# Loading q and k in longer runs, two batches per transfer, with both heads' scores over 128 rows of contraction

## Chip, core and metric

The kernel runs on one core of one Trainium2 chip. The metric is the time of one execution on the device, in microseconds (us); lower is better. TensorE multiplies matrices into PSUM; VectorE and ScalarE move results from PSUM to SBUF and compute on them; GpSimd issues nearly all loads from HBM, and SyncE the rest.

## What is computed

Selective attention over 8 batches of 8 heads, 576 tokens, 64 channels a head, and on its result a spectral mixing layer. All inputs are float32. Cut to what matters:

```python
# attention, per batch and head: q, k, v are [576, 64], s is [576]
scores = q @ k.T / 8
cum = np.cumsum(np.maximum(s, 0.0))
scores = np.where(causal, -1e9, scores + np.minimum(-(cum[:, None] - cum[None, :]), 0.0))
attn = softmax(scores)
x[b, :, 64 * head : 64 * head + 64] = attn @ v

# mixing, per batch: x is [576, 512], 64 modes, each with two 512x512 weights
X = rfft(x, axis=tokens)[:64]
Y = X @ (w_r + 1j * w_i)              # a matrix for each mode
u = x + irfft(Y)
out = u + np.maximum(u @ w_ch, 0.0)
```

The weights are the bulk of what is read: 2 x 64 matrices of 512x512. The type is converted from float32 to bfloat16 or float16 by the load itself, so that a load writes half of the bytes that it reads.

## The kernel before

**Steps.** Attention runs in 32 steps n. A step is one batch b and one pair of heads g (n = 8 g + b). What a step needs is loaded ahead: q and k of both heads, and v. The lists of loads are written in program order, one list per step: list n holds q, k and v of step n + 3 (`LA = 3`) and about five tiles of mixing weights. `load` merges the two kinds evenly into one order, and GpSimd issues them one after another. A weight tile is two transfers of 256 KB (bytes written), one for each half of the 128 partitions (L214). The first eight weight tiles lie in buffers that are needed for something else only later; the others go round two rings of 11 and 6 buffers (`WA`, `WB`; from tile 76 on the ring of 11 alone). A weight tile may be loaded when the matmuls that read the tile before it in its buffer are over.

**q and k.** `loads_qkv(n)` loads q in one transfer into `q2`, [128 partitions, 9 tokens, 64 channels]: each head takes 64 partitions, and a partition holds a run of 9 tokens, 1152 bytes as bfloat16. k goes to `k2` in the same way. The pool holds four such pairs.

**Transposes.** The scores need q and k with the channels on the partitions. `transposes(n, 0)` does q of both heads, `transposes(n, 1)` k: 9 x 2 TensorE transposes of 64x64 into one PSUM tile (there is one, so that the second call waits for the copies of the first), then two copies of 64x576 into SBUF. Head A's channels land in rows 0 to 63 of `qtA`, `ktA`, head B's in rows 64 to 127 of `qtB`, `ktB`. Three of the four copies are on VectorE, the last (`ktB`) on ScalarE (L335). There are two buffers of each, used in turn.

**Scores.** The bias enters as one more row of contraction: row 64 of `qtA` and row 0 of `qtB` hold minus 8 times the running sum (`cum_rows`, two small loads on SyncE's queue per step), and the same row of `ktA`, `ktB` holds ones. Head A contracts over 65 rows, head B over 128, of which 63 are zeros. `scores(n, h)` first adds the causal mask by a matmul (L368), then the products (L374), and ScalarE takes the exponential (L382). `scores4` does the last 64 tokens of both heads.

**The rest of a step.** `av` multiplies with v and divides by the row sums (x_all), `fft` transforms along the tokens, and `modes` multiplies with the weights (L452), one group of four weight tiles at a time, in steps 8 and later. The order of work on TensorE in step n is

```python
cum_rows(n + 1)
scores(n, 0); av(n - 1, 1); transposes(n + 1, 0)
scores(n, 1); transposes(n + 1, 1); fft(n - 1); av(n, 0)
for c in mode_steps.get(n, []): modes(...)
```

with products with `w_ch` among it in the last six steps. After attention come the remaining weights of the last channel group, with `modes` as they land, and then the inverse transform, the product with `w_ch`, relu and the stores.

Of the kernel before, what the change touches and what calls it, by code (L numbers as in the profile page):

```python
# [11 lines left out]
BF16 = mybir.dt.bfloat16  # L12
# [6 lines left out]
def kernel(  # L19
# [11 lines left out]
    nc = tc.nc  # L31
# [3 lines left out]
    P = 128  # L35
# [15 lines left out]
    NF = NT - 1  # L51
    R = S // (P // 2)
    RP = P // 2
    W = 2 * P
# [58 lines left out]
    ap_ = at.enter_context(tc.tile_pool(name="attn", bufs=1))  # L113
    qkpool = at.enter_context(tc.tile_pool(name="qk_sb", bufs=LA + 1))
    cumt_sb = ap_.tile([P, NK + 1, NPAIR], FP32, name="cumt_sb")
    cumt4 = ap_.tile([P, NPAIR // 2], FP32, name="cumt4")
    ncum_sb = ap_.tile([NPAIR, S], BF16, name="ncum_sb")
    NQ = 2
    qtA = [ap_.tile([NCH, S], BF16, name=f"qtA{i}") for i in range(NQ)]
    qtB = [ap_.tile([P, S], BF16, name=f"qtB{i}") for i in range(NQ)]  # L120
    ktA = [ap_.tile([NCH, S], BF16, name=f"ktA{i}") for i in range(NQ)]
    ktB = [ap_.tile([P, S], BF16, name=f"ktB{i}") for i in range(NQ)]
    NV = LA + 2
# [22 lines left out]

    def loads_qkv(n):

        if n >= N:
            return []  # L150
        g, b = divmod(n, B)
        hs = slice(2 * g, 2 * g + 2)
        q2 = qkpool.tile([P, R + 1, D], BF16, name="q2", tag="q2")[:, :R, :]
        k2 = qkpool.tile([P, R + 1, D], BF16, name="k2", tag="k2")[:, :R, :]
        loaded[n] = (q2, k2)
        todo = [
            (dst, src[b, hs].rearrange("h (p r) d -> (h p) r d", r=R))
            for src, dst in ((q, q2), (k, k2))
        ]
        todo += [  # L160
            (
                v2[n % NV][:, : 2 * NWN * W].rearrange("p (w h c) -> p w h c", w=NWN, h=2)[:, :, h, P:],
                v[b, 2 * g + h, : NF * P, :].rearrange("(w p r) d -> p w (r d)", p=P, r=2),
            )
            for h in range(2)
        ]
        return todo

# [85 lines left out]
    nc.sync.dma_start(out=negm32, in_=d_negm)  # L254
    first, second, tails0 = loads_qkv(0), loads_qkv(1), loads_tails(0)
    load(first[:2])
    load(loads_w(W0), first[2:] + tails0 + second)
    nc.sync.dma_start(out=Ff_sb, in_=d_Ff.rearrange("(T p) c -> p T c", p=P))
# [6 lines left out]
    for i in range(NQ):  # L265
        nc.vector.memset(qtB[i][0:64, :], 0.0)
        nc.vector.memset(ktB[i][0:64, :], 0.0)
        nc.vector.memset(ktB[i][0:1, :], 1.0)
        nc.vector.memset(ktA[i][D : D + 1, :], 1.0)
    for i in range(NV):  # L270
# [44 lines left out]
    def cum_rows(n):  # L315
        if n >= N:
            return
        g, b = divmod(n, B)
        p0 = b * H + 2 * g
        nc.sync.dma_start(out=qtA[n % NQ][D : D + 1, :], in_=ncum_sb[p0 : p0 + 1, :])  # L320
        nc.sync.dma_start(out=qtB[n % NQ][0:1, :], in_=ncum_sb[p0 + 1 : p0 + 2, :])

    def transposes(n, which):
        if n >= N:
            return
        src = loaded[n][which]
        dA, dB = ((qtA, qtB), (ktA, ktB))[which]
        g, b = divmod(n, B)
        ps = trpool.tile([P, R, RP], BF16, name="tr_ps", tag="tr")
        for r in range(R):  # L330
            for h in range(2):
                rows = slice(D * h, D * h + D)
                nc.tensor.transpose(ps[rows, r, :], src[rows, r, :], ident16[rows, rows])  # L333
        for dst, rows in ((dA, slice(0, D)), (dB, slice(D, P))):
            copy = (nc.vector.tensor_copy, nc.scalar.copy)[which == 1 and dst is dB]  # L335
            copy(  # L336
                out=dst[n % NQ][rows, :].rearrange("d (p r) -> d p r", r=R),
                in_=ps[rows].rearrange("d r p -> d p r"),
            )

    def scores4(n, ps):
# [5 lines left out]
        )  # L347
        for h, (kt, qt) in enumerate(((ktA, qtA), (ktB, qtB))):
            nc.tensor.matmul(  # L349
                ps[NL * h : NL * h + NL, :], kt[n % NQ][:, i0:], qt[n % NQ][:, i0:],  # L350
                start=False, stop=True, skip_group_check=True,
            )
# [5 lines left out]
    def scores(n, h):  # L358
        g, b = divmod(n, B)
        pidx = b * H + 2 * g + h  # L360
        qt = (qtA, qtB)[h][n % NQ]
        pt = p_sb[(2 * n + h) % NP_]
        keys = (ktA, ktB)[h][n % NQ][:, : NF * P].rearrange("c (w p r) -> c w r p", p=P, r=2)
        for r in range(2):
# [7 lines left out]
            for w, i0, i1 in ((0, 0, 512), (0, 512, S), (1, W, S)):  # L372
                c0 = w * S + i0 - w * W
                nc.tensor.matmul(  # L374
                    ps[:, c0 : c0 + i1 - i0], keys[:, w, r, :], qt[:, i0:i1],
                    start=False, stop=True, skip_group_check=True,
                )
# [163 lines left out]
    with tc.tile_pool(name="sc_psum", bufs=2, space=PSUM) as scpool, \  # L541
# [4 lines left out]
        transposes(0, 1)  # L546
        load(loads_qkv(2))
        pad_p()
        for n in range(N):
            if n in (0, 2):  # L550
                nc.vector.memset(xs_flat[n // 2].bitcast(FP32), 0.0)
            tails_due = loads_tails(n // B + 1)[n % B - 3 : n % B - 2] if 2 < n % B < 5 else []
            load(loads_qkv(n + LA) + tails_due, loads_w(on_chip[n]))
            cum_rows(n + 1)
# [375 lines left out]
```

## Time and profile before

| | |
|---|---|
| time, median of 7 runs | 448.5 us (447.7 to 450.46) |
| the profiled execution | 449.35 us; its span from first to last instruction 447.4 us |
| TensorE busy | 352.6 us, 4697 matmuls |
| VectorE, ScalarE busy | 251.5 us, 218.7 us |
| GpSimd busy, nearly all of it issuing loads | 259.7 us |
| mean granted TensorE clock | 0.894 |
| DMA | 77251 packets, 93.30 MB written |
| read from HBM | 163.51 MB |
| attention, from the first to the last transposes of q and k | 10.9 to 322.3 us |
| last weights landed | about 411 us |

How to read the profile: it is one execution, its times in us from the first instruction. The page shows the span in 40 equal slices with the busy share of each engine, of the 16 DMA engines together, and what they moved in GB/s (bytes written). The list of waits says who waited for whom: us in all, times, the longest. A line of the timeline is start, us, engine, line, operation, what it writes and reads, and in brackets the idle time of the engine before it and what ended that ("issue": nothing that the profile shows). A group of instructions is line, engine, operation, out<-in, count | us busy, mean ns of one | idle time before them, and who ended it. The DMA view of a stretch gives packets, bytes and the mean rate, and for each queue packets, MB and the time of its packets as a share of 16 engines; q0 holds what GpSimd issued. L226 is the line that issues loads of q, k, v and weights; a buffer's name in the profile stands for all of its copies (`qtA` for both).

### The profile page before, as it was taken

Reading aid. Unit: us, or ns where it says so; the run is one execution under the profiler, and the core shown is the slowest. Engines: PE = TensorE matmul, PEld = TensorE weight load, DVE = VectorE, ACT = ScalarE, POOL = GpSimd, SP = SyncE. Lnnn points to the kernel's source line nnn. Section 1 sums busy time; section 2 is a strip of 40 time slices with the busy share of each in tenths; the row PEclk is TensorE's granted clock in tenths of the full one; section 3 lists DMA queues with packets and bytes.
Section 4 is the critical chain, followed back from the end, with each engine's and each line's share of the span. In section 5 each row is a group of like instructions: output and inputs, shape, how many; then the busy total and the mean of one; then the engine's idle time right before and its main releaser. Section 6 shows DMA issues by size and latency. Waiting matters only on the chain.

```text
span 447.4 us, 11460 instructions
## 1 busy us (share of the span) xinstructions
PE 352.6 (79%) x4697; PEld 222.1 (50%) x4729; DVE 251.5 (56%) x576; ACT 218.7 (49%) x387; POOL 259.7 (58%) x405
## 2 busy tenths in 40 slices
PE   1798988997554979986868876879987997769994
PEld 0466666565333645663446544546654455333341
DVE  6675776674333644764436445446665554442885
ACT  1485778465324653664246345546650344221583
POOL 6866665765566666555575656566644545430393
PEclk9996999997688876998569889889998899979998
DMA  9999999999999999999999999999999999996598
GB/s 176 199 196 205 204 204 205 188 205 207 207 207 204 203 188 193 209 207 206 206 199 205 206 207 207 207 205 205 200 209 211 209 210 209 210 218 136 171 353 345
DMA packets 77251, 93.30 MB, mean 209 GB/s; under 512 B 30144, under 2 KB 39872, under 8 KB 77200
## 3 DMA queue, kind: packets, MB, share of 16 engines
q0 software_dynamic: 67984, 81.29, 105.4%
q1 hardware_dynamic: 9216, 11.29, 7.8%
q8 instruction: 37, 0.61, 0.5%
q14 instruction: 14, 0.11, 0.1%
HBM read 163.51 MB, written 9.44 MB: 387 GB/s over the span
## 4 chain that ended last, share of the span: by engine, by line
DMA 64%; PE 18%; issue 6%; POOL 5%; DVE 5%; POOLq 1%; SPq 0%; ACT 0%; DVEq 0%
DMA w_sb<-in_moe_w_i_dram 30%; DMA w_sb<-in_moe_w_r_dram 18%; DMA q<-in_q_dram 8%; DMA k<-in_k_dram 6%; PE sc_ps L374 3%; PE av_ps L403 3%; POOL r_w L766 3%; PE sc_ps L368 2%; PE ft_ps L429 2%; PE tr_ps L333 2%; PE yp L452 2%; PE z_ps L624 2%; POOL w_sb L226 1%; DMA qtA<-ncum_sb 1%; DMA xs<-c_negm 1%
## 5 line engine op out<-in xcount | busy, mean ns | idle before, releaser
L382 ACT ACTIVATE p_sb<-sc_ps,cumt_sb 128x576 f16<-128x576 f32 (+1 forms) x256 | 142.0, 636 | 59.3 <-PE sc_ps L374 58.8
L226 POOL DMA_DIRECT2D w_sb<-in_moe_w_r_dram x120 | 71.6, 597 | 61.9 <-DMA w_sb<-in_moe_w_r_dram 19.3
L226 POOL DMA_DIRECT2D w_sb<-in_moe_w_i_dram x120 | 71.4, 596 | 47.1 <-DMA w_sb<-in_moe_w_i_dram 15.8
L226 POOL DMA_DIRECT2D v<-in_v_dram x72 | 51.7, 719 | 23.9 <-DMA w_sb<-in_moe_w_i_dram 7.1
L368 PE MATMUL sc_ps<-negm,ident 128*128 128x256 bf16 x256 | 56.4, 307 | 0.2
L452 PE MATMUL yp<-w_sb,xs 128*32 128x512 bf16 (+1 forms) x480 | 44.4, 445 | 9.4 <-DMA w_sb<-in_moe_w_i_dram 3.1
L403 PE MATMUL av_ps<-v,p_sb 128*128 128x65 f16 x1024 | 45.4, 199 | 0.0
L333 PE MATMUL tr_ps<-ident,q 64*64 64x64 bf16 x576 | 17.3, 209 | 35.3 <-DMA q<-in_q_dram 35.3
L336 DVE COPY ktA<-tr_ps 64x576 bf16<-64x576 bf16 x32 | 24.0, 749 | 34.7 <-PE tr_ps L333 34.7
L403 PEld LDWEIGHTS <-p_sb 128*128 128x128 f16 x1024 | 39.5, 101 | 5.2 <-DVE x_all L413 2.1
L336 DVE COPY qtA<-tr_ps 64x576 bf16<-64x576 bf16 x32 | 23.8, 744 | 31.4 <-PE tr_ps L333 31.4
L374 PE MATMUL sc_ps<-qtA,ktA 65*128 65x512 bf16 (+2 forms) x192 | 37.9, 308 | 0.7 <-DMA qtA<-ncum_sb 0.7
L353 ACT ACTIVATE p<-sc_ps,cumt 128x64 f16<-128x64 f32 x32 | 10.1, 314 | 56.9 <-PE sc_ps L349 56.9
L374 PE MATMUL sc_ps<-qtB,ktB 128*128 128x64 bf16 (+2 forms) x160 | 33.8, 315 | 3.3 <-issue 2.2
L439 DVE CAST xs<-ft_ps 64x128 bf16<-64x128 f32 x128 | 31.5, 284 | 8.2 <-PE ft_ps L429 7.7
L408 DVE TENSOR_REDUCE den<-av_ps 128x5 f32<-128x10 f32 x64 | 10.8, 169 | 43.0 <-PE av_ps L403 42.1
L429 PE MATMUL ft_ps<-Ff_sb,x_all 128*64 128x96 f16 (+1 forms) x640 | 33.0, 224 | 1.0 <-DVE x_all L413 1.0
L452 PEld LDWEIGHTS <-xs 128*32 128x32 bf16 (+1 forms) x512 | 19.8, 146 | 27.5 <-issue 17.3
L413 DVE TENSOR_TENSOR x_all<-av_ps,rcp 128x320 f16<-128x320 f32 x64 | 31.4, 491 | 2.2
L333 PEld LDWEIGHTS <-q 64*64 64x64 bf16 x576 | 13.5, 122 | 37.9 <-DMA q<-in_q_dram 36.8
L333 PE MATMUL tr_ps<-ident,k 64*64 64x64 bf16 x576 | 16.2, 202 | 20.0 <-DVE qtB L336 8.8
L336 ACT COPY ktB<-tr_ps 64x576 bf16<-64x576 bf16 x32 | 20.3, 634 | 23.8 <-DVE ktA L336 22.8
(119 smaller groups left out, 555.1 us busy)
## 6 DMA issues: line engine op xcount, KB each, us to landing
w_sb<-in_moe_w_r_dram POOLq DMA_DIRECT2D x120, 256.0 KB, 7.9
w_sb<-in_moe_w_i_dram POOLq DMA_DIRECT2D x117, 256.0 KB, 8.2
out_dram<-r_w SPq DMA_DIRECT2D x14, 512.0 KB, 3.0
q<-in_q_dram POOLq DMA_DIRECT2D x32, 144.0 KB, 7.2
k<-in_k_dram POOLq DMA_DIRECT2D x32, 144.0 KB, 7.3
v<-in_v_dram POOLq DMA_DIRECT2D x72, 64.0 KB, 6.9
x_all<-in_moe_w_i_dram POOLq DMA_DIRECT2D x6, 256.0 KB, 7.3
out_dram<-r_w SPq DMA_DIRECT2D x6, 256.0 KB, 3.2
```

The costliest lines, as they stand in the source:

```text
L226: nc.gpsimd.dma_start(out=dst, in_=src)
L333: nc.tensor.transpose(ps[rows, r, :], src[rows, r, :], ident16[rows, rows])
L336: copy(out=dst[n % NQ][rows, :].rearrange("d (p r) -> d p r", r=R), in_=ps[rows].rearrange("d r p -> d p r"),)
L368: nc.tensor.matmul(ps[:, bass.ds(w * S, W)], ident16, negm[:, bass.ts(r, W)], start=True, stop=False, skip_group_check=True,)
L374: nc.tensor.matmul(ps[:, c0 : c0 + i1 - i0], keys[:, w, r, :], qt[:, i0:i1], start=False, stop=True, skip_group_check=True,)
L382: nc.scalar.activation(out=pt[:, poff[x] : poff[x] + S - w * W], in_=ps[:, w * S : (w + 1) * S - w * W], func=ACTF.Exp, bias=cumt_sb[:, x, ...
L403: nc.tensor.matmul(ps[:, I, r : r + NCH], lhsT, rhs, start=(i == 0), stop=(i == len(todo) - 1), skip_group_check=True,)
L413: nc.vector.tensor_tensor(out=x_all[:, g, b, :, D * h : D * h + D], in0=ps[:, :, 1 : NCH], in1=rcp.unsqueeze(2).to_broadcast([P, NT, D]), ...
L429: nc.tensor.matmul(ps[HP * h : HP * h + HP, q_, :], x_all[:nT, g, b, T, q_::2], Ff_sb[:nT, T, 3 * HM * h : 3 * HM * (h + 1)], start=(T == ...
L439: nc.vector.tensor_copy(out=xs[g % 2][rows, :, k, h, :, b, :], in_=ps[rows, :, k * HM : (k + 2) * HM].rearrange("p q (r m) -> p q r m", r=2),)
L452: nc.tensor.matmul(ps[32 * cg : 32 * cg + 32, :], cols[k0:, q_, 1 - ri, :, c * MC // 2 + cg], wt[(g, c, ri, cg // 2)][k0:, 2 * (cg % 2) + ...
L766: nc.gpsimd.tensor_tensor(out=rs[i], in0=rs[i], in1=z1s[i], op=ALU.add)
```

## The change

q and k are loaded in runs of 18 tokens instead of 9: a head takes 32 partitions of a tile, both heads 64. q takes the lower 64 partitions and k the upper 64 of one tile `qk2`, which holds two batches (the steps n and n + 1, n even). So one transfer brings q of two steps, and one k, each into 64 partitions in 128 runs of 2304 bytes; for the first two steps each batch has its own transfers. They stand in the lists of odd steps; v keeps its place, as `loads_v`. Two such tiles take the place of four pairs.

A call of `transposes` now does half of the tokens of a run (9 of 18) of q and of k, both heads at once, and its two copies spread the 9 tokens over the 18 of each run: q's stays in rows 0 to 63, k's goes from rows 64 to 127 to rows 0 to 63. Three copies are on VectorE, the last (k, second half) on ScalarE, as before. The transposed q and k of both heads lie side by side in `qt` and `kt`, channels in rows 0 to 63, the bias in row 64 and zeros below it, so that both heads contract over 128 rows.

```diff
-    R = S // (P // 2)
-    RP = P // 2
+    RP = P // 4
+    R = S // RP
+    RH = R // 2
...
-    qkpool = at.enter_context(tc.tile_pool(name="qk_sb", bufs=LA + 1))
+    qkpool = at.enter_context(tc.tile_pool(name="qk_sb", bufs=2))
...
-    qtA = [ap_.tile([NCH, S], BF16, name=f"qtA{i}") for i in range(NQ)]
-    qtB = [ap_.tile([P, S], BF16, name=f"qtB{i}") for i in range(NQ)]
-    ktA = [ap_.tile([NCH, S], BF16, name=f"ktA{i}") for i in range(NQ)]
-    ktB = [ap_.tile([P, S], BF16, name=f"ktB{i}") for i in range(NQ)]
+    qt = [ap_.tile([P, 2, S], BF16, name=f"qt{i}") for i in range(NQ)]
+    kt = [ap_.tile([P, 2, S], BF16, name=f"kt{i}") for i in range(NQ)]
...
-    def loads_qkv(n):
+    def loads_qk(n):
...
-        q2 = qkpool.tile([P, R + 1, D], BF16, name="q2", tag="q2")[:, :R, :]
-        k2 = qkpool.tile([P, R + 1, D], BF16, name="k2", tag="k2")[:, :R, :]
-        loaded[n] = (q2, k2)
-        todo = [
-            (dst, src[b, hs].rearrange("h (p r) d -> (h p) r d", r=R))
-            for src, dst in ((q, q2), (k, k2))
+        t = loaded[n] = loaded[n + 1] = qkpool.tile([P, 2, R * D], BF16, name="qk2", tag="qk2")
+        return [
+            (
+                t[HP * i : HP * i + HP, x0:x1],
+                src[b + x0 : b + x1, hs].rearrange("b h (p r) d -> (h p) b (r d)", r=R),
+            )
+            for x0, x1 in ([(0, 2)] if n else [(0, 1), (1, 2)])
+            for i, src in enumerate((q, k))
         ]
...
-    first, second, tails0 = loads_qkv(0), loads_qkv(1), loads_tails(0)
+    first = loads_qk(0)
     load(first[:2])
-    load(loads_w(W0), first[2:] + tails0 + second)
+    load(loads_w(W0), loads_v(0) + loads_tails(0) + first[2:] + loads_v(1))
...
-        nc.vector.memset(qtB[i][0:64, :], 0.0)
-        nc.vector.memset(ktB[i][0:64, :], 0.0)
-        nc.vector.memset(ktB[i][0:1, :], 1.0)
-        nc.vector.memset(ktA[i][D : D + 1, :], 1.0)
+        nc.vector.memset(qt[i][D:], 0.0)
+        nc.vector.memset(kt[i][D:], 0.0)
+        nc.vector.memset(kt[i][D : D + 1], 1.0)
...
-    def transposes(n, which):
+    def transposes(n, half):
...
-        ps = trpool.tile([P, R, RP], BF16, name="tr_ps", tag="tr")
-        for r in range(R):
-            for h in range(2):
-                rows = slice(D * h, D * h + D)
+        src = loaded[n][:, n % 2, :].rearrange("p (r d) -> p r d", d=D)[:, half * RH : half * RH + RH]
+        ps = trpool.tile([P, RH, 2 * RP], BF16, name="tr_ps", tag="tr")
+        for r in range(RH):
+            for i in range(2):
+                rows = slice(HP * i, HP * i + HP)
                 nc.tensor.transpose(ps[rows, r, :], src[rows, r, :], ident16[rows, rows])
-        for dst, rows in ((dA, slice(0, D)), (dB, slice(D, P))):
-            copy = (nc.vector.tensor_copy, nc.scalar.copy)[which == 1 and dst is dB]
+        for i, dst in enumerate((qt, kt)):
+            copy = (nc.vector.tensor_copy, nc.scalar.copy)[half * i]
+            to = dst[n % NQ][:D].rearrange("d h (p r) -> d h p r", r=R)
             copy(
-                out=dst[n % NQ][rows, :].rearrange("d (p r) -> d p r", r=R),
-                in_=ps[rows].rearrange("d r p -> d p r"),
+                out=to[:, :, :, half * RH : half * RH + RH],
+                in_=ps[HP * i : HP * i + HP].rearrange("d r (h p) -> d h p r", h=2),
             )
...
-        keys = (ktA, ktB)[h][n % NQ][:, : NF * P].rearrange("c (w p r) -> c w r p", p=P, r=2)
+        keys = kt[n % NQ][:, h, : NF * P].rearrange("c (w p r) -> c w r p", p=P, r=2)
...
-        load(loads_qkv(2))
+        load(loads_qk(2) + loads_v(2))
...
-            load(loads_qkv(n + LA) + tails_due, loads_w(on_chip[n]))
+            load((loads_qk(n + LA) if n % 2 else []) + loads_v(n + LA) + tails_due, loads_w(on_chip[n]))
```

`cum_rows` loads the two bias rows to row 64 of `qt`, one per head, and `scores4` and `scores` take `qt[:, h]` and `kt[:, h]`.

## The prediction

> **What bounds the kernel now.** I read the page first: what moves data, and what the chain that ended last is made of.
>
> ```profile
> DMA  9999999999999999999999999999999999996598
> GB/s 176 199 196 205 204 204 205 188 205 207 207 207 204 203 188 193 209 207 206 206 199 205 206 207 207 207 205 205 200 209 211 209 210 209 210 218 136 171 353 345
> DMA 64%; PE 18%; issue 6%; POOL 5%; DVE 5%; POOLq 1%; SPq 0%; ACT 0%; DVEq 0%
> ```
>
> The DMA engines are full for 36 of 40 slices (to about 411 us), at 199 to 211 GB/s written but for a few dips; the last 36 us are TensorE, VectorE and GpSimd work that the change doesn't touch. Second view, the waits:
>
> ```profile
> PE tr_ps L333 <- DMA q<-in_q_dram: 37.8, 15, 6.0
> PE tr_ps L333 <- DMA k<-in_k_dram: 8.6, 6, 2.4
> ```
>
> It is tempting to count these 46 us as time that earlier q and k would give back. But TensorE waits because the DMA stream is full. Does the stream ever wait for TensorE? In the timeline of GpSimd, which issues all loads, a DMA waits for the landing of the one issued eight before it. Its longest pauses during attention are these two, which follow no such landing and no release of a buffer that I can find:
>
> ```profile
> 79.36 0.60 POOL L226 DMA_DIRECT2D w_sb<-in_moe_w_r_dram  x1 [1.79 <-issue]
> 163.83 0.60 POOL L226 DMA_DIRECT2D w_sb<-in_moe_w_r_dram  x1 [2.78 <-issue]
> ```
>
> So the stream runs freely, and I price the change by what it does to the stream. Third view, the DMA view of five stretches: 320 to 391 us (weights alone), 185 to 225 (all kinds mixed), 9 to 320, and the two dips 80 to 87 and 164 to 172.
>
> ```profile
> DMA packets 8145, 14.89 MB, mean 210 GB/s; under 512 B 922, under 2 KB 922, under 8 KB 8137
> q0 software_dynamic: 8105, 14.75, 111.5%
> ```
> ```profile
> DMA packets 6747, 8.26 MB, mean 207 GB/s; under 512 B 2678, under 2 KB 3318, under 8 KB 6742
> q0 software_dynamic: 6486, 8.18, 116.7%
> ```
> ```profile
> DMA packets 59318, 63.12 MB, mean 203 GB/s; under 512 B 27314, under 2 KB 35792, under 8 KB 59277
> ```
> ```profile
> DMA packets 1145, 1.25 MB, mean 178 GB/s; under 512 B 478, under 2 KB 720, under 8 KB 1144
> ```
> ```profile
> DMA packets 995, 1.38 MB, mean 173 GB/s; under 512 B 243, under 2 KB 466, under 8 KB 993
> ```
>
> **Price of a packet.** Let a MB cost a and a packet b. Weights alone: 71 = 14.89 a + 8145 b. Mixed: 40 = 8.26 a + 6747 b. The first times 8.26/14.89 gives 39.39 = 8.26 a + 4518 b; the difference is 0.61 = 2229 b, so b = 0.28 ns over all 16 engines together (4.4 ns on one), and a = 4.615 us per MB. The stretch 265 to 293 us (4541 packets, 5.79 MB) gives the same 0.28.
>
> **Term 1, fewer packets: -1.3 us.** q and k are 64 transfers of 128 packets of 1152 B, and become 34: 30 of 128 packets of 2304 B, and four of 64 packets for the first pair. That is 8192 data packets down to 4096, the bytes being the same. Each transfer also ends in 16 four-byte packets; 30 transfers fewer save 480. 4576 x 0.28 ns = 1.28 us, all on the stream that sets the end. Bounds: nothing, if the packets are cut up again; and from the shares, where packets overlap: 1266.6 engine-us for 14.75 MB and 8105 packets against 746.9 for 8.18 MB and 6486 give 22 ns a packet on one engine, 4576 x 22 / 16 = 6.3 us. I take 1.3, because it comes from the stretches' own clock; the shares add to over 100%, so much of the 22 ns lies under the next packet.
>
> **Term 2, the dips: -0.5 us.** By a and b, 9 to 320 us needs 63.12 x 4.615 + 59318 x 0.00028 = 307.9 of its 311 us: 3.1 us idle. The two dips hold 0.9 (7 - 6.1) and 1.35 (8 - 6.65) of that: GpSimd paused, and the eight transfers in flight ran short. A list of loads is now 144 + 144 + 64 + 64 KB and about ten weight halves of 256 KB, 213 KB each, eight of them 8.1 us of stream by a. Two lists after: 576 + 256 + 5120 KB in 26 transfers, 229 KB each, 8.7 us. This cushion of 0.6 us could take up to 0.6 from each dip; but where the pauses fall will shift, since there are fewer instructions before them. I take half, 0.5; the ends are -2.2 (both gone) and +1 (a pause that meets the small v transfers).
>
> **What I cost at nothing, and its cover.**
> Transposes and copies keep number and size: 18 transposes and two 64x576 copies per call, three on VectorE and one on ScalarE per step. Their outputs change to runs of nine elements, k's moved from the upper 64 rows to the lower:
>
> ```profile
> L336 DVE COPY qtA<-tr_ps 64x576 bf16<-64x576 bf16 x32 | 23.8, 744 | 31.4 <-PE tr_ps L333 31.4
> L439 DVE CAST xs<-ft_ps 64x128 bf16<-64x128 f32 x128 | 31.5, 284 | 8.2 <-PE ft_ps L429 7.7
> ```
>
> L439 writes four runs of 32, and (744 - 284)/448 = 1.03 ns per further element: the runs add nothing visible. L684 takes 690 ns for 512 elements moved across rows half of the time. No row has runs as short as nine; I take 0, between -0.1 and +0.75 us a copy.
> Score matmuls of head A get 128 rows for 65: medians in the view of L374 are 298 and 300 ns for the two heads. Nothing.
> A new wait: scores of head 0 need ScalarE's k copy, not only VectorE's. At n=1 it ends 0.6 us after the scores began (23.11 against 22.59); near 72 us it ends 0.3 before (72.60 against 72.94). Behind the waiting matmul stand all of TensorE's later work, av(n-1,1) first, and that head's exponentials on ScalarE.
> The second wait: the first transposes of an even step need the whole k pair, a quarter list (about 3.6 us) later than q, plus the doubled transfers; odd steps wait for nothing. So TensorE runs two steps per wait, some 4 us late in even ones.
> Third: two pair buffers for four. The pair for steps 4 and 5 is issued at 23.8; the transposes that free its buffer end at 21.6. Later the margin is 5 us and more.
> All three are covered by TensorE's lead over the stream. Early, the first 25 weight tiles have places of their own; the 51st weight transfer, issued at 93.8, is the first to overwrite a tile, whose last matmul ended at 83.9 and its group's at 84.8: 9 us. The narrowest place is late, where the second of these lines overwrites what the first has read:
>
> ```profile
> 326.34 1.09 PE L452 MATMUL yp<-w_sb,xs 128*32 128x512 bf16 x16 [1.18 <-DVE z L516]
> 328.31 0.59 POOL L226 DMA_DIRECT2D w_sb<-in_moe_w_i_dram  x1 [0.88 <-DMA w_sb<-in_moe_w_i_dram]
> ```
>
> That is 0.9 us; behind it stands the queue in flight, 9.7 us from issue to landing there, where the shortest landing of any load is 3.9: 5.8 more. If this cover goes, every us of lateness beyond 6.7 is a us of the end.
> The moved step: in odd lists GpSimd issues 1.4 us of transfer for the second batch a list earlier, ahead of weights; the tightest weight is issued at 87.6, used at 98.9 and lands in 8, so 3 us cover it. SP issues two rows per step as before.
> The start: four zero fills of 298 ns double, +1.2 us; VectorE sat idle 1.19 us just before L279, waiting for the mask. The two rows of ones, twice as long, replace four.
>
> **A rule against the change.** Each q and k transfer now fills 64 partitions, where it filled 128; but each weight transfer fills 64 as well (L214), and the stretch of weights alone is the fastest, 210 GB/s. By the row: 0. The Trainium skill, "SBUF — State Buffer", section "Door 1: The DMA port swizzle", says that 64 partitions reach only half of the 16 ports, 196 against 328 GB/s at 1 MiB. As an estimate by that page, the 9.4 MB of q and k at 210 GB/s, 45 us, would grow to 75, and the sum to +28 us; no row here supports it.
>
> **Sum.** -1.3 - 0.5 = -1.8 us. The profiled execution took 449.35 us (span 447.4, 1.95 around it): 447.6. It stood 0.85 above the median of 448.5, so the median becomes 446.7.
>
> **Rivals.** (A measurement of this kernel can tell about 0.3%, 1.35 us, from no change: 447.15 to 449.85.)
> No gain: packets over 4096 B read are cut up; the longest weight packet reads 4096 B, the new one 4608. Then only the 480 end packets (0.13 us) and the dips remain: 447.9, between 447.2 and 449.5. Chance 0.25.
> Slower: the copies with nine-element runs cost 1.5 us instead of 0.75. VectorE's three per step add 2.2 us; over steps 0 to 7 that is 18 us of lateness against a margin of 93.8 - 84.8 = 9 and a cushion of 3.3 (7.2 from issue to landing less 3.9): 5.7 us idle at about 90 us, 448.5 + 5.7 - 1.3 = 452.9. It decides from about 1.25 us a copy (12.3/8 = 1.5 per step). For it: no row with such runs. Against: L439. With milder forms, 450 to 455, chance 0.18.
> More: all idle time goes, -3.1 - 1.3: 444.1. Not more, since the stream has no more idle time, whatever TensorE waits. Chance 0.1.
>
> **How the numbers follow.** The forecast, 445.4 to 447.9, has 0.47. Faster by over 0.3%: four fifths of it and the last rival and some of the second, 0.5; same: 0.3; slower: 0.2. The range leaves out the slowest forms and the last bit of the best: 444.6 to 450.6.
>
> **What would show it.** Right: packets fall from 77251 to about 72700; the mixed stretches run at about 208 GB/s; the last weight lands about 2 us earlier; q's wait for odd steps vanishes while TensorE's total wait stays. Wrong: as many packets; copies over 0.8 us; GpSimd pausing for TensorE; a stretch of attention under 200 GB/s beyond two dips.

## The result, and the profile after

| | before | after |
|---|---|---|
| median of the first comparison | 448.29 us (447.09 to 450.46, 32 runs) | 446.7 us (446.16 to 448.14, 13 runs) |
| ratio, 95% interval | | 0.9964 [0.9953, 0.9975] |
| the same in two later comparisons | 448.15, 448.02 us | 447.2, 446.85 us: 0.9974 [0.9959, 0.9988], 0.9975 [0.9961, 0.9990] |
| profiled execution (its span) | 449.35 us (447.4) | 446.7 us (444.7) |

By the three ratios the change gains 1.1 to 1.6 us, 0.25 to 0.36%. Two further profiles of after have spans of 444.8 and 444.5 us; the profiled execution of before stood about 1.1 us above the median of its kernel, so that the two profiles lie 2.7 us apart and not 1.5. That has to be kept in mind below wherever profiles are compared.

The page after: rates of the 40 slices, and the chain.

```profile
GB/s 183 202 206 205 205 206 205 206 202 207 207 209 201 201 207 187 205 206 208 207 202 206 208 208 205 208 206 203 205 209 209 211 210 208 209 218 128 175 352 344
DMA 51%; PE 25%; DVE 8%; POOL 6%; issue 6%; ACT 3%; POOLq 1%; DVEq 0%; ACTq 0%
```

The stream of loads is still full and still holds most of the chain, though less of it (DMA 51% for 64%). The dip of the eighth slice (188 GB/s before) is gone, those of the 15th and 16th (188, 193) are one (187). The waits:

```profile
PE tr_ps L336 <- DMA qk<-in_k_dram: 28.7, 9, 5.0
PE tr_ps L336 <- DMA qk<-in_q_dram: 25.2, 6, 10.9
POOL w_sb L232 <- PE yp L456: 11.8, 9, 2.2
```

TensorE waits for q and k 15 times where it waited 21 times, but for 53.9 us in all where it was 46.4: once per pair, longer each time. This is the reading that the prediction warned of: the wait that an engine shows is not time that can be had. The last row was small in before: GpSimd now waits 11.8 us, and not 1.8, for TensorE's products before it may load over a weight tile. The line of before:

```profile
POOL w_sb L226 <- PE yp L452: 1.8, 3, 0.7
```

The DMA view of 9 to 320 us and of the stretch of the former dip, 80 to 87 us:

```profile
DMA packets 55055, 63.67 MB, mean 205 GB/s; under 512 B 26744, under 2 KB 27262, under 8 KB 55014
```
```profile
DMA packets 1229, 1.44 MB, mean 205 GB/s; under 512 B 614, under 2 KB 614, under 8 KB 1228
```

In the same 311 us it moves 0.55 MB more in 4263 fewer packets. The last weights in the chain of waits, after:

```profile
398.11 10.35 DMA w_sb<-in_moe_w_i_dram
408.50 0.67 PE yp L456 x4
```

The first line ends at 408.46. In the chain of before it is this line, which ends at 411.16:

```profile
400.76 10.40 DMA w_sb<-in_moe_w_i_dram
```

2.7 us earlier, as much as the spans differ: what is gained is gained in the stream, and the tail is as long as it was (36.2 us).

### The profile page after: what moved, and what is told of

Same layout as the page of the kernel before. It is cut to its first block, busy times and chain, and to the rows that moved or that the text cites. A ratio compares the mean times of both kernels' runs of the same rounds, so it can differ in the third digit from the quotient of the medians.

```text
span 444.7 us, 11399 instructions
## 1 busy us (share of the span) xinstructions
PE 340.4 (77%) x4697; PEld 217.8 (49%) x4729; DVE 251.3 (57%) x574; ACT 221.3 (50%) x387; POOL 243.0 (55%) x375
## 2 busy tenths in 40 slices
DMA packets 72675, 93.30 MB, mean 210 GB/s; under 512 B 29664, under 2 KB 31200, under 8 KB 72624
## 4 chain that ended last, share of the span: by engine, by line
DMA 51%; PE 25%; DVE 8%; POOL 6%; issue 6%; ACT 3%; POOLq 1%; DVEq 0%; ACTq 0%
DMA w_sb<-in_moe_w_i_dram 20%; DMA w_sb<-in_moe_w_r_dram 19%; DMA qk<-in_k_dram 10%; PE yp L456 4%; PE z_ps L628 4%; PE sc_ps L378 3%; POOL r_w L770 3%; PE ft_ps L433 2%; PE av_ps L407 2%; DMA x_all<-in_moe_w_r_dram 2%; PE z_ps L539 2%; POOL w_sb L232 2%; PE tr_ps L336 2%; PE sc_ps L372 2%; DVE qt L340 1%
## 5 line engine op out<-in xcount | busy, mean ns | idle before, releaser
L340 DVE COPY qt<-tr_ps 64x576 bf16<-64x576 bf16 x64 | 47.8, 747 | 76.3 <-PE tr_ps L336 76.3
L336 PE MATMUL tr_ps<-ident,qk 64*64 64x64 bf16 x1152 | 34.8, 204 | 65.7 <-DMA qk<-in_k_dram 28.7
L378 PE MATMUL sc_ps<-qt,kt 128*128 128x64 bf16 (+2 forms) x352 | 70.6, 309 | 4.3 <-ACT kt L340 2.2
L336 PEld LDWEIGHTS <-qk 64*64 64x64 bf16 x1152 | 26.4, 117 | 76.0 <-DMA qk<-in_k_dram 29.7
L372 PE MATMUL sc_ps<-negm,ident 128*128 128x256 bf16 x256 | 54.1, 296 | 0.2
L378 PEld LDWEIGHTS <-kt 128*128 128x128 bf16 x384 | 40.5, 106 | 26.3 <-issue 5.7
L456 PE MATMUL yp<-w_sb,xs 128*32 128x512 bf16 (+1 forms) x480 | 37.3, 398 | 8.8 <-DMA w_sb<-in_moe_w_i_dram 2.1
L340 ACT COPY kt<-tr_ps 64x576 bf16<-64x576 bf16 x32 | 23.0, 718 | 15.1 <-DVE qt L340 14.3
L433 PEld LDWEIGHTS <-x_all 128*64 128x64 f16 (+1 forms) x640 | 22.1, 111 | 8.7 <-DVE x_all L417 1.1
L628 PE MATMUL z_ps<-wch_sb,xs 128*128 128x512 f16 x96 | 24.9, 406 | 0.2 <-DVE xs L622 0.2
```

The costliest lines, as they stand in the source:

```text
L340: copy(out=to[:, :, :, half * RH : half * RH + RH], in_=ps[HP * i : HP * i + HP].rearrange("d r (h p) -> d h p r", h=2),)
L372: nc.tensor.matmul(ps[:, bass.ds(w * S, W)], ident16, negm[:, bass.ts(r, W)], start=True, stop=False, skip_group_check=True,)
L378: nc.tensor.matmul(ps[:, c0 : c0 + i1 - i0], keys[:, w, r, :], qh[:, i0:i1], start=False, stop=True, skip_group_check=True,)
L433: nc.tensor.matmul(ps[HP * h : HP * h + HP, q_, :], x_all[:nT, g, b, T, q_::2], Ff_sb[:nT, T, 3 * HM * h : 3 * HM * (h + 1)], start=(T == ...
L456: nc.tensor.matmul(ps[32 * cg : 32 * cg + 32, :], cols[k0:, q_, 1 - ri, :, c * MC // 2 + cg], wt[(g, c, ri, cg // 2)][k0:, 2 * (cg % 2) + ...
L628: nc.tensor.matmul(z[:, x, :], xts[i][:, x, dt, :], wch_sb[:, dt, :], start=(dt == 0), stop=(last and dt == DT - 1), skip_group_check=True,)
```

## What the packets cost, and how full the queue is

Two things could make the stream shorter: fewer packets (term 1 of the prediction) and less idle time while GpSimd pauses (term 2). A third theory has to be set against both: that the new arrangement of transposes, copies and scores, which changes TensorE's and VectorE's work, brought the gain. The first four kernels keep the compute part of after and change only how q and k come in. "Control" is after itself.

> The changed kernel again, beside the next three on the same chip, as their common base. Both theories: 446.7 us, about 1.6 us (0.36%) under the kernel before.

Measured: 447.2 us, ratio 0.9974 [0.9959, 0.9988].

**Every batch its own transfers.**

```diff
-            for x0, x1 in ([(0, 2)] if n else [(0, 1), (1, 2)])
+            for x0, x1 in [(0, 1), (1, 2)]
```

> The changed kernel, but q and k of every batch in transfers of their own: 64 transfers of 64 packets for 34; the data packets stay 4096 of 2304 B, and 480 end packets come back (73155 in all). Theory 'packets on a full stream': 480 x 0.28 ns = +0.13 us, so 446.8 us. Theory 'queue in flight' (the larger transfers fill the pauses of GpSimd): up to +0.5 us, 447.3 us, the dips of the stream deeper. Rival 'TensorE's timing' (the pair that arrives at once, or the order of the loads, made the gain): back to about 448 us, with data packets as few as after.

Measured: 448.41 us, ratio 1.0016 [0.9994, 1.0039]; 1.2 us over the control (0.8 to 2.7, resampling the runs of both). The whole gain is gone, though the data packets are as few as after and the compute part is untouched. So neither the packets alone nor TensorE's part alone makes the gain; the 30 transfers saved are worth more than the predicted 0.13 to 0.63 us. The profiled execution took 450.08 us, 1.7 us above this median; in it the last weight landed at 411.34 us, 2.9 us later than in after, and TensorE's last products ended 1.0 us behind it (for 0.7), at a lowered clock (see the last experiment of the section on the cover).

**Runs of 9 tokens, runs of 3 tokens**, in these 64 transfers, into the same 64 partitions:

```diff
-        t = loaded[n] = loaded[n + 1] = qkpool.tile([P, 2, R * D], BF16, name="qk2", tag="qk2")
+        t = loaded[n] = loaded[n + 1] = qkpool.tile([P, 2, 2, 640], BF16, name="qk2", tag="qk2")[:, :, :, : 9 * D]
...
-                t[HP * i : HP * i + HP, x0:x1],
-                src[b + x0 : b + x1, hs].rearrange("b h (p r) d -> (h p) b (r d)", r=R),
+                t[HP * i : HP * i + HP, x],
+                src[b + x, hs].rearrange("h (p y r) d -> (h p) y (r d)", y=2, r=9),
```

(for runs of 3: a tile [P, 2, 6, 256] and y=6, r=3).

> As the kernel with 64 transfers, but each partition's 18 tokens lie in two places of the tile, so that they come as two runs of 9 tokens: 8192 data packets of 1152 B (as before the change), into the same 64 partitions, with the same transposes, copies and scores as after. Theory 'packets on a full stream': 4096 x 0.28 ns = +1.15 us on top of the 64 transfers, about 448.0 us, within 0.3 us of the kernel before; the stretches of mixed loads slower, the stretch of weights alone unchanged. Rival 'TensorE's timing' or 'the layout of q and k': no more than the kernel with 64 transfers takes, 446.8 us.

Measured: 448.81 us, ratio 1.0018 [0.9999, 1.0038]; 0.4 us over the kernel with 64 transfers (-1.3 to 1.3): too small to be told apart from either theory. The last weights of the two kernels' profiles landed at 411.53 and 411.34 us.

> As the kernel with 64 transfers, but in six runs of 3 tokens a partition: 24576 data packets of 384 B, 20480 more. Theory 'packets on a full stream' at the price of the prediction: 20480 x 0.28 ns = +5.7 us over the kernel with 64 transfers, about 452.5 us; at the upper bound of the prediction (22 ns a packet on one engine) +28 us, 475 us. If the price is not per packet but rises for short ones (384 B), something above 452.5 that the run with 9 tokens does not show. Rival 'bytes alone': 446.8 us, since the bytes are the same.

Measured: 451.16 us, ratio 1.0067 [1.0043, 1.0091]; 2.75 us over the kernel with 64 transfers (1.2 to 3.4). Packets do cost time, but less than half of the 5.7 us. The DMA view of 30 to 70 us, taken as a full stretch in both, of after and of the kernel with runs of 3:

```profile
DMA packets 7979, 8.20 MB, mean 205 GB/s; under 512 B 4476, under 2 KB 4476, under 8 KB 7972
```
```profile
DMA packets 11065, 8.06 MB, mean 201 GB/s; under 512 B 8282, under 2 KB 8282, under 8 KB 11058
```

With a per MB and b per packet, as in the prediction: 40 = 8.20 a + 7979 b and 40 = 8.06 a + 11065 b. The first times 8.06/8.20 is 39.317 = 8.06 a + 7843 b; the difference, 0.683 = 3222 b, gives b = 0.21 ns over 16 engines (between 0.20 and 0.23 by the rounding of the MB) and a = 4.67 us per MB. So in this stretch a packet costs 0.21 ns and not 0.28; 20480 of them 4.3 us. In time they cost 2.75 us, 0.13 ns each. The rest of the sum tells part of why. If a and b hold everywhere, what 9 to 320 us needs by them, against its 311 us, leaves the time in which the stream stood idle:

| kernel | packets, MB in 9 to 320 us | idle, us |
|---|---|---|
| before | 59318, 63.12 | 3.5 |
| after; two more profiles of it | 55055, 63.67 | 1.9; 1.6, 1.2 |
| 64 transfers | 55323, 63.10 | 4.5 |
| 64 transfers, runs of 9 | 59398, 63.11 | 3.6 |
| 64 transfers, runs of 3 | 75012, 62.85 | 1.5 |
| before with pairs (below), twice | 59069, 63.58 | 1.4, 0.7 |
| v cut in two (below) | 53853, 61.04 | 14.4 |

For after: 311 - 63.67 x 4.672 - 55055 x 0.000212 = 1.9. The stream with the most packets is slower and idles less: of 4.3 us of packets 3.0 came back as idle time in the two profiles. With the time measured this fits only roughly: 1.3 us are left of 2.75, and the two profiled executions lie 1.7 us above and 0.8 us below the medians of their kernels. And in the table the kernels with two batches per transfer and v uncut idle 0.7 to 1.9 us, those without, but for the one just named, idle 3.5 to 4.5.

**Does the queue run short?** The theory of the prediction's term 2 was that GpSimd's pauses empty the eight transfers in flight, and that larger transfers cover more of a pause. To see it large, v's transfers, the smallest, are cut in two:

```diff
-                v2[n % NV][:, : 2 * NWN * W].rearrange("p (w h c) -> p w h c", w=NWN, h=2)[:, :, h, P:],
-                v[b, 2 * g + h, : NF * P, :].rearrange("(w p r) d -> p w (r d)", p=P, r=2),
+                v2[n % NV][:, : 2 * NWN * W].rearrange("p (w h c) -> p w h c", w=NWN, h=2)[:, w, h, P:],
+                v[b, 2 * g + h, : NF * P, :].rearrange("(w p r) d -> p w (r d)", p=P, r=2)[:, w],
             )
             for h in range(2)
+            for w in range(NWN)
```

The "fit" named in this and two later expectations was made over the profiles then at hand; its working is not shown here. Its 0.22 ns for a data packet agrees with the 0.21 above. Its 1.2 ns for an end packet can't be told from a queue that runs short, and is not used further.

> The changed kernel with each transfer of v (64 KB) cut into two of 32 KB: 64 more transfers, 1024 more end packets, as many data packets. By the prediction's price (0.28 ns for any packet): +0.3 us. By the fit (1.2 ns for an end packet): +1.2 us. If a transfer costs what the split of q and k into 64 transfers showed (1.2 to 1.6 us for 30, so 40 to 50 ns each, most of it because the queue of eight transfers holds fewer bytes when GpSimd pauses): +2.6 to +3.2 us.

Measured: 460.79 us, ratio 1.0294 [1.0275, 1.0313]: 13.9 us over the control of the same comparison, four times the largest of the three forecasts. DMA issues of 9 to 320 us (operation, count, KB each, median us from issue to landing), of before, after, and v cut in two:

```profile
w_sb<-in_moe_w_r_dram POOLq DMA_DIRECT2D x88, 256.0 KB, 7.6
```
```profile
w_sb<-in_moe_w_r_dram POOLq DMA_DIRECT2D x90, 256.0 KB, 8.2
```
```profile
w_sb<-in_moe_w_r_dram POOLq DMA_DIRECT2D x84, 256.0 KB, 6.9
v<-in_v_dram POOLq DMA_DIRECT2D x120, 32.0 KB, 6.0
```

The last column is the depth of the queue in time, since a load is issued when the one eight before it has landed (in these three traces 0.3 us after it at the least, 0.4 to 0.5 us in the middle). Eight transfers of before hold 7.6 us, of after 8.2: the 0.6 us that the prediction worked out. With v cut in two it is 6.9. The gain from 7.6 to 8.2 is of the order of 1 us, the loss from 8.2 to 6.9 is 13.9: the cost rises steeply as the queue gets shallow. The windows of that kernel (us; the last column is GB/s):

```profile
9.00:80.00 71.00, 58.12 (x946) 40.98 (x956) 46.01 (x124) 45.45 (x85) 50.61 (x87) 0.93 1.21 195
80.00:160.00 80.00, 53.02 (x895) 36.39 (x900) 39.76 (x100) 38.03 (x72) 48.79 (x84) 0.89 1.16 196
160.00:240.00 80.00, 59.38 (x973) 40.60 (x984) 41.11 (x104) 40.76 (x76) 48.68 (x83) 0.84 1.14 193
```

The loss lies in every stretch of attention (205, 205 and 203 after; in 240 to 320 us it is 202 for 206), and not only at GpSimd's long pauses. The last line of the fence before says what is short: a transfer of 32 KB holds its place among the eight for 6.0 us, nearly as long as one of 256 KB, and by a it brings 0.15 us of stream instead of 1.2. There is a second way in which small transfers can starve the stream: GpSimd needs 0.6 us to issue one. In 9 to 320 us it still waited 79 us for landings (87 after), so the eight places still hold it up; but 40% of its loads were issued with more than one place free (14% after). Both may play a part, and no run here separates them.

What follows, by the medians: the size of the transfers, through the depth of a queue of eight, is the larger part of what the change gains (1.2 us); the packets are the smaller (0.4 us between runs of 18 and of 9 tokens, which is within the noise).

## One part of the change alone: the pairs

The kernel before, with its own runs of 9 tokens, 128 partitions, transposes and scores; only the loads are grouped:

```diff
+            for x0, x1 in ([(0, 2)] if n else [(0, 1), (1, 2)])
...
-            load(loads_qkv(n + LA) + tails_due, loads_w(on_chip[n]))
+            load((loads_qk(n + LA) if n % 2 else []) + loads_v(n + LA) + tails_due, loads_w(on_chip[n]))
```

> The kernel before (runs of 9 tokens, 128 partitions, its own transposes, copies and scores) with one part of the change alone: two batches per transfer, in the lists of odd steps, two pair buffers: 34 transfers of q and k for 64, 8192 data packets as before. Theory 'packets on a full stream': only the 480 end packets, -0.13 us. Theory 'queue in flight': up to -0.5 us more, 447.7 us where the kernel before takes 448.3. Rival 'the pairs make the gain': 446.7 us, as the whole change.

Measured: 448.22 us, ratio 1.0002 [0.9988, 1.0015]. No gain, although the last weight landed at 409.09. So it ran again beside the control:

> The changed kernel once more, on one chip with the next three, as their base: 446.7 to 447.2 us, ratio to the kernel before 0.9964 to 0.9974 as in the two comparisons so far.

Measured: 446.85 us, ratio 0.9975 [0.9961, 0.9990].

> The kernel before with two batches per transfer alone, again, because its first comparison (ratio 1.0002) and its profile disagree: there the last weight landed 2.1 us earlier than in the profile of before, and 1.2 us of that went to a longer wait for the last output store. Theory 'additive' (0.22 ns for a data packet, 1.2 ns for an end packet, as a fit of full stretches of nine profiles gives them): 480 x 1.2 ns = -0.6 us, and what the runs of 18 tokens add is 4096 x 0.22 ns = -0.9 us: 447.6 us, between before and after. Rival 'only both together': 448.2 us again, with the last store as late again.

Measured: 447.95 us, ratio 1.0000 [0.9989, 1.0011]; 1.1 us over the control (0.6 to 1.7). In its second profile the last weight lands at 408.46, as in after:

```profile
397.73 10.73 DMA w_sb<-in_moe_w_i_dram
```

Yet its span is 445.9 us and not 444.7. From the last weight to the last instruction of the chain's arithmetic the two are alike; the difference is in the stores of the result. DMA issues of 428 us to the end, after and then the pairs alone:

```profile
out_dram<-r_w SPq DMA_DIRECT2D x9, 512.0 KB, 3.0
```
```profile
out_dram<-r_w SPq DMA_DIRECT2D x10, 512.0 KB, 4.2
```

In the last 17 us the stores run one behind the other at about 400 GB/s, so that 1.2 us lost once stays to the end. Both profiles of this kernel show it (4.1 and 4.2 us); before has 3.0, the three of after 3.0, 2.9 and 3.4 us. What holds the stores up there I could not settle. As a time, the rival "only both together" is what was measured. The profiles say that the pairs do their work on the stream and that this kernel loses it in its last stores; why, and whether q and k have a part in that, is not shown. The packets, too, show little at the end of the stream: with 4096 more of them it ends at 409.09 and 408.46 us, in the three profiles of after at 408.46, 408.33 and 407.72, 0.6 us earlier in the mean.

## The cover: VectorE's copies and TensorE's transposes

**Copies twice**, for the rival that ended on the slow side:

```diff
-            copy(
+            for _ in range(1 if half * i else 2):
+              copy(
```

> The changed kernel with each of VectorE's three copies of transposed q and k issued twice, as if they took 1.5 us instead of 0.75: +2.25 us of VectorE's time per step, 72 us in all. By the prediction's rival: lateness of 18 us over steps 0 to 7 against a cover of 12.3: +5.7 us, 452.4 us, with GpSimd waiting at about 90 us for TensorE's reads of weight tiles. If VectorE has slack inside a step, or the cover is larger, less than +1 us; if the copies stand on the chain in every step, far more, up to +72 us.

Measured: 477.87 us, ratio 1.064 [1.060, 1.068]: +31 us. Its waits:

```profile
PE tr_ps L336 <- DVE kt L341: 66.0, 32, 3.5
POOL w_sb L232 <- PE yp L457: 54.6, 14, 12.7
POOL qk L232 <- PE tr_ps L336: 17.6, 5, 5.7
```

The longest wait of GpSimd is near the place that the prediction gave, the first weight tiles that are overwritten (93.8 us before):

```profile
108.97 0.59 POOL L232 DMA_DIRECT2D w_sb<-in_moe_w_r_dram  x1 [12.71 <-PE yp L457]
```

But the price was wrong by a factor of five (5.7 us). The prediction counted the lateness of steps 0 to 7 against the cover and stopped. The lateness of a step comes again in every step: 32 x 2.25 = 72 us are added, TensorE's waits for q and k (53.9 us after) can take in at most those, and at least 18 us are left over. No wait of TensorE for q or k is left in its list of waits, so that all of the 53.9 us was used up. Where the rest up to 31 us comes from, these runs do not show.

**Transposes twice:**

```diff
-        for r in range(RH):
+        for r in [*range(RH)] * 2:
```

> The changed kernel with every transpose of q and k done twice on TensorE: about +1 us of TensorE's time per step, 30 us in all. Theory 'the full stream sets the end, TensorE only fills its waits for q and k' (54 us in the changed kernel): within 1 us of 446.7, its waits for q and k shorter by about as much as the work is longer; what there is of loss comes at the end of attention, where GpSimd already waits for TensorE's reads of weights (316 to 336 us), as transfers started later. Rival 'TensorE's time makes the difference of the kernels': up to +30 us, 476 us.

Measured: 448.1 us, ratio 0.9997 [0.9984, 1.0009], some 1.2 us over after. The doubled transposes took 19.8 us more of TensorE (54.6 for 34.8 us busy), the waits for q and k fell by 8.2:

```profile
PE tr_ps L336 <- DMA qk<-in_k_dram: 23.6, 7, 4.9
PE tr_ps L336 <- DMA qk<-in_q_dram: 22.1, 5, 8.7
POOL w_sb L232 <- PE yp L456: 15.4, 9, 3.4
```

So 20 us of work on the engine with the most waiting cost 1.2 us: TensorE's time is worth little here. But 1.2 is not nothing, and where it goes is not shown. GpSimd waits 3.6 us longer for TensorE's products (15.4 for 11.8, the last row). The profiled execution, however, took 450.26 us, 2.2 us above the median, and it ended late for another reason: its last weight landed at 409.39 us, and TensorE began its last products only at 411.83, behind products slowed by the clock as in the next experiment.

**The copies' engines changed over**, for ScalarE's copy that became 84 ns longer:

```diff
-            copy = (nc.vector.tensor_copy, nc.scalar.copy)[half * i]
+            copy = (nc.vector.tensor_copy, nc.scalar.copy)[half * (1 - i)]
```

> One look at the 84 ns that ScalarE's copy of k became longer (718 ns for 634): the second half's two copies change engines, q's (rows 0 to 63 to rows 0 to 63) on ScalarE and k's (rows 64 to 127 to rows 0 to 63) on VectorE. If the shift of rows costs ScalarE the 84 ns: q's copy there 634 ns. If the runs of nine elements do: 718 ns as k's. VectorE's k copy stays at 763 ns. The time stays at 446.7 within 0.5 us in either case.

The groups (line, engine, operation, out<-in, count, us busy, mean ns) of before for ScalarE, then of after, then of this kernel:

```profile
L336 ACT COPY ktB<-tr_ps 64x576 bf16<-64x576 bf16 x32 | 20.3, 634 | 23.8 <-DVE ktA L336 22.8
```

```profile
L340 DVE COPY qt<-tr_ps 64x576 bf16<-64x576 bf16 x64 | 47.8, 747 | 76.3 <-PE tr_ps L336 76.3
L340 DVE COPY kt<-tr_ps 64x576 bf16<-64x576 bf16 x32 | 24.4, 763 | 0.4
L340 ACT COPY kt<-tr_ps 64x576 bf16<-64x576 bf16 x32 | 23.0, 718 | 15.1 <-DVE qt L340 14.3
```
```profile
L340 ACT COPY qt<-tr_ps 64x576 bf16<-64x576 bf16 x32 | 22.7, 709 | 12.1 <-PE tr_ps L336 12.1
DVE kt L340 <- ACT qt L340: 64.0, 32, 3.1
```

Without a shift of rows ScalarE still takes 709 ns, so that 75 of the 84 ns come with the runs of nine, and 9 with the shift. VectorE's copies show none of it (747 and 763 ns, 744 to 761 before). The time was a miss: the one run took 449.69 us, some 2.7 us more than after. Its last weight landed at 408.59, as early as in after, but TensorE was the later one. Its chain, and that of a second profile of after (the control), at the same eight products with `w_ch` and at the last products:

```profile
402.11 3.59 PE z_ps L628 x8
411.61 0.60 PE yp L456 x4
```
```profile
401.22 2.21 PE z_ps L628 x8
408.71 0.60 PE yp L456 x4
```

Of the 2.9 us between the two, 0.9 were there when the eight products began. VectorE's copy of k, which now waits 64 us in all for ScalarE's of q (the second row of the fence before), is a likely reason for these. The other 2.0 us were lost from there on: the eight products took 3.59 us for 2.21. The window of 400 to 412 us shows why; the third number from the end is the granted clock, for this kernel and for the control:

```profile
400.00:412.00 12.00, 11.07 (x53) 4.12 (x50) 3.27 (x5) 0.59 (x2) 0.00 (x0) 0.72 0.75 152
400.00:412.00 12.00, 10.94 (x64) 4.63 (x63) 3.85 (x8) 1.29 (x3) 0.00 (x0) 0.92 0.62 129
```

In windows of 2 us it is 0.50 here from 400 to 406 us and 0.79 in the next, 1.00 before and after: by that it stood at half for 6.8 us. In the three profiles of after it did so for 3.4 us, and earlier (between 396 and 402), so that fewer products fell into it. The profiled executions of the doubled transposes and of the 64 transfers have 6.8 us at the same place as here, and their eight products took 3.58 us each. What lowers the clock there, and how often for how long in the other executions, no run shows.

In the control TensorE is the later one too, if by 0.3 us: the last weight had landed at 408.33, and its products could have begun at once. In the other two profiles of after the stream ended last, at 408.46 and 407.72 us. So the end of the stream and the end of TensorE's work of the last groups lie close together in the changed kernel, and a faster stream alone may gain little; how much is not shown.

## The two bias rows in one transfer

Fewer, larger transfers helped; SyncE's two bias rows per step can be one transfer:

```diff
-        for h in range(2):
-            nc.sync.dma_start(out=qt[n % NQ][D : D + 1, h, :], in_=ncum_sb[p0 + h : p0 + h + 1, :])
+        nc.sync.dma_start(out=qt[n % NQ][D : D + 1, :, :], in_=ncum_sb[p0 : p0 + 2, :])
```

> The changed kernel with SyncE's two loads of bias rows per step made one (32 fewer transfers of 1152 B, 512 fewer end packets): what the price of end packets points to as a next step. By the fit, -0.6 us: 446.2 us; by the prediction's price, -0.14 us. If the stream no longer sets the end alone (one profile of the changed kernel has TensorE's last products 0.2 us behind the last weight), less than half of that shows.

Measured: 446.26 us, ratio to before 0.9964 [0.9952, 0.9977]; 0.6 us under the control beside it (-1.1 to +0.2). It is ahead of before for certain and of after by the median only; the packets fall by 1920, from 72675 to 70755, where 512 were expected. In 30 to 70 us a row alone is 32 packets (352 for 11 transfers in after), both rows together are 4 (24 for 6).

## Why the prediction was right, point by point

The time forecast was 446.7 us, and 446.7 was measured. What bounds the kernel and both mechanisms were right, but the two terms were mis-sized, one too large and one too small, and a cost of the compute part may have been missed. That the sum met the first measurement to a tenth is luck: it says -1.8 us, and the three comparisons gave 1.1 to 1.6 us.

- **What bounds the kernel: right.** The spans differ by as much as the landings of the last weight, 2.7 us in the profiles; 20 us of added work on TensorE cost 1.2.
- **Number of packets: right.** 72675 forecast as about 72700; so the rival "packets cut at 4096 B read" falls.
- **Term 1, -1.3 us: too large.** At 0.21 ns instead of 0.28, 4576 packets are 1.0 us; in time still less was seen, 0.4 us (-1.3 to 1.3) between runs of 18 and of 9 tokens, and 0.13 ns a packet for the runs of 3. Weights alone against mixed loads, from which the 0.28 came, differ in more than packets: at 0.21 ns the 2229 packets are 0.47 of the 0.61 us that carried the whole price, and the other 0.14 is that the weights alone run faster (71 us where a and b give 71.3; the mixed stretch 40 where they give 40.0). The upper bound of 6.3 us, from the shares, was far off.
- **Term 2, -0.5 us: the mechanism right, the size too small.** The depth of the queue grew by the 0.6 us forecast, but what it is worth was taken as half of 0.6 for two dips. Splitting the pairs again cost 1.2 us (0.8 to 2.7), of which 480 x 0.21 ns = 0.1 is packets; so the term is about -1.1. By a and b the two dips held 2.3 of the 3.5 us that before stood idle. In after the first is gone, and the second has moved to 172 to 180 us, behind a pause of GpSimd of 2.3 us up to 174.1; it holds 0.9 to 1.1 us in the three profiles. With 64 transfers 0.9 us lie there and 1.4 in 266 to 280 us, at another pause, out of 4.5. So much of the idle time lies at pauses, but not all, and not each pause costs: before pauses 2.4 us up to 247.1, longer than one of the two pauses that the prediction calls the longest, and the stream runs at 207 GB/s through it (244 to 252 us).
- **The compute part at nothing: open.** With packets and transfers as before, but the new transposes, copies and scores, the kernel with runs of 9 tokens took 1.0018 [0.9999, 1.0038] of before: 0 to 1.7 us more, which is not clear of the noise. By the medians of that comparison the three steps from before to after are +0.7 (compute part), -0.4 (runs of 18) and -1.2 (pairs), -0.95 in all; the first two are each smaller than what their ranges leave open. Where a cost of the compute part would arise, no profile here shows.
- **Copies: right for VectorE,** 747 and 763 ns; ScalarE's grew by 84 ns, inside the range that the prediction gave, though not at its 0. What that costs in time, no run shows.
- **The new waits: right.** The wait of scores for ScalarE's copy is two waits of 2.2 us in all (`PE sc_ps L378 <- ACT kt L340`). No load of q or k waited for TensorE's transposes in the list of waits, so two pair buffers suffice. TensorE waits once per pair.
- **The narrowest place: right as a place.** At 327 us GpSimd waited there for TensorE, in the timeline:

```profile
326.05 1.09 PE L456 MATMUL yp<-w_sb,xs 128*32 128x512 bf16 x16 [1.18 <-DVE z L520]
327.00 1.18 POOL L232 DMA_DIRECT2D w_sb<-in_moe_w_i_dram  x2 [2.18 <-PE yp L456]
```

  "GpSimd pausing for TensorE" was named as a sign of being wrong. It came, and the stream did not suffer: 320 to 400 us ran at 211 GB/s before and after.
- **The slower rival: its threshold untested, its price wrong.** With VectorE's copies issued twice, 1.5 us for each, the kernel takes 478 us, not 452.9. The step that failed is the sum over steps 0 to 7; a cost that comes in every step has to be set against the slack of all steps.
- **The rule on 64 partitions: the choice of the row was right.** The kernel with runs of 9 has before's packets and transfers, into 64 partitions for 128, and takes 1.0018 [0.9999, 1.0038] of its time. In 30 to 70 us it moves

```profile
DMA packets 8385, 8.18 MB, mean 204 GB/s; under 512 B 4146, under 2 KB 5552, under 8 KB 8378
```

  which is before's rate there, 204 GB/s with 8643 packets. The rule of the Trainium skill, "SBUF — State Buffer", section "Door 1: The DMA port swizzle", would have cost some 30 us by the prediction's estimate; at the 200 to 210 GB/s of these converting loads, eight in flight, no run shows any of it. What a single transfer into 64 partitions reaches was not measured here.

## What to carry to other kernels

On a full stream of loads count transfers before packets: see how long a load takes from issue to landing, compare that with the pauses and the issue time of the engine that feeds the queue, and put the smallest transfers together first. A wait of an engine that follows the stream is slack and not a gain to be had; but a cost that comes in every step eats that slack in every step, so its price is at least the sum over all steps less all of the slack (18 of the 31 us of the copies). When a term of a few tenths of a per cent decides, take two profiles of each kernel: the one of before lay 1.1 us off its median, that of the doubled transposes 2.2, as much as the whole gain and more.

## What the runs showed of the hardware that was not expected

- A packet costs 0.21 ns over 16 engines, 3.4 ns on one of them, in a stretch taken as full; in the time of the kernel 20480 of them cost 0.13 ns each. The Trainium skill, "DMA: Bandwidth & Descriptors", section "Why small descriptors are slow (HBM only)", gives about 3 cycles per packet; if they are cycles of the 850 MHz of that page's section "Where 436 GB/s comes from", that is 3.5 ns as an estimate, which agrees with the full stretch.
- 64 more transfers of half the size, the data the same, cost 13.9 us of 447. At 0.21 ns their 1024 end packets are 0.2 us of it; the rest is a stream that is fed too slowly.
- ScalarE's copy of 64x576 from PSUM takes 634 ns into a row without gaps and 709 to 718 ns into runs of nine with gaps; VectorE's takes 744 to 763 ns into either.
- The mean granted TensorE clock hides what matters at the end. It is 0.909 to 0.923 in the profiles of the exchanged copies (one run), the 64 transfers and the doubled transposes, and 0.898 to 0.913 in the three of after. But by windows of 2 us from 394 to 412 us the clock stands at half for 6.8 us in the first and for 3.4 us in the others (6.8 in before and none with the bias rows in one transfer; these profiles have nothing between). With the exchanged copies and the doubled transposes TensorE's last products begin 3.0 and 2.4 us after the last weight.
